# Ten of sixteen weight decodings of a second layer set beside the attention pairs, and a new room for four weights

## The chip, the cores and the metric

The kernel runs on one core of one Trainium2 chip. The metric is the device time of one execution in microseconds (us). Three executions of the kernel before took 651.32, 652.01 and 653.17 us; the median is 652.01 us. "A change of 0.3%" is about 2 us here.

## The reference

The program computes a causal attention with a compressive memory and then a two-layer network on its output.

```python
# q, k, v: (4, 8, 576, 64)   k is scaled by 8, z_prev by 8
scores = q @ k.T / 8, causal;  a = softmax(scores);  local = a @ v
q_p = elu(q) + 1
mem_out = (q_p @ M_prev) / (q_p . z_prev + 1e-6)
x = g * mem_out + (1 - g) * local          # g = sigmoid(beta), per head
x -> (2304 tokens, 512)
h = x @ w_in                               # (512, 2048)
out = (h * sigmoid(1.702 * h)) @ w_out     # (2048, 512)
```

Both weight matrices are 64-bit floats in memory. The kernel reads them as pairs of 32-bit words and decodes them to 32-bit floats on the chip.

## The kernel before, in words

**Stage one: pairs beside the first layer.** A pair is one batch index and two heads, so there are 16 pairs. `plan_prep` and `plan_attend` enter each step of a pair into a table of slots (`at(slot, priority, fn)`); `step()` runs one slot's entries and then issues matmuls of the first layer (`first_moe`) until the slot has its share of TensorE time (`PACE`). Pairs are 7 slots apart at first and 8 later: `K0` is 0, 7, 14, 21, 29, 37, ..., 61 for pair 8, ..., 117 for pair 15. The program text is then ordered again by a scheduler that simulates the engines' time and takes, per engine, what it believes is ready, by priority in order of text; an instruction can so stand earlier in its engine's queue than in the text. Each engine runs its queue in order.

The first layer runs over eight chunks of tokens (`chunks`: 256 and 320 columns for each batch index) and, in each chunk, over 16 blocks of 128 hidden units. A block is 12 matmuls (four of depth 128, each with a high and a low part of the weight and a low part of the activation). `gate` copies a finished block from PSUM into an SBUF tile `hk` (three buffers) and stores it into a scratch tensor `gd` in DRAM; the copies are ScalarE's in the late part, and alternate between VectorE and ScalarE before. Chunk 7's input tiles `xh`, `xl` lie in the pool `mop`.

**Decoding a weight block** of 128x512 numbers takes one load of 512 KB (`wraw`), one ScalarE scaling (`scale`), three VectorE bit operations (`bits`) and, later, a split in a high and a low part. First-layer weights are decoded by `conv_unit` (loads on SyncE's DMA queue), the second layer's by `conv_pair` (loads on GpSimd's DMA queue). A second-layer weight `wo` number kk (0 to 7) is made of two blocks, kk and kk+8; `sums` forms four sums and differences of their halves (tile `st`), `w_hi` copies raw halves and sums to the high part on ScalarE (three instructions), `w_lo` subtracts to get the low part on VectorE (three instructions). The seven products of a Strassen step use these parts. In the kernel before all sixteen blocks are decoded after the last pair, in the loop `while fill["gen"] is not None or conv_q or events`, beside the first layer's last chunks; weights 0 to 4 get their split in that loop, weights 5 to 7 after it.

**Stage two: the second layer.** `units` lists 84 units: three groups of 768 tokens, seven products, four parts p. Unit n needs weights 2p and 2p+1 and one tile `g` of activations: `load_g` loads 384 KB from `gd` on SyncE's queue, `gelu` applies the activation on ScalarE, `split` makes `oh` (ScalarE) and `ol` (VectorE) from it, `product` issues 12 matmuls. The first four units use tiles g[1,1] (p = 0 to 3), the next four g[0,0], then g[1,0], then g[0,1]. Two of the g[1,1] tiles have room of their own (`g11a`) and are loaded in the loop (k = 18 and 20).

**Room.** Pools stack up from two sides of SBUF in the order in which they are opened; a pool opened after another was closed takes its room, and a tile in it waits until the tiles that lay there are done. `left.close()` frees `mop` (23.75 KB in each partition), `cnv` (8 KB of raw words), and the first layer's 16 weights (4 KB each). On that room the second layer's pools are opened: in the kernel before g10 (12 KB), g01 (12), weights 5, 6, 7 (14 each), g11b (6), opb (6), g00 (12).

## Time and profile before

| | |
|---|---|
| profiled execution | 655.16 us, of which the span of its instructions is 653.1 us |
| median of three executions | 652.01 us |
| TensorE (PE) busy | 603.1 us, 92% of the span, 4000 matmuls |
| VectorE (DVE) busy | 417.1 us, 64% |
| ScalarE (ACT) busy | 355.2 us, 54% |
| GpSimd (POOL) busy | 164.0 us, 25% |
| mean granted TensorE clock | 0.98 |

The stages by the clock of the trace: first queries until about 45 us; pairs beside the first layer until 388 us; the first layer's rest until 450 us; the second layer to 648 us. Engines run their own queues in order, so an idle stretch of an engine is read by what ended it ("<-"). PEclk is the granted TensorE clock, 1.00 for 2.4 GHz and 0.50 for 1.2 GHz. Matmul ends are modelled, and neighbouring matmuls overlap in the rows; the start times are used for counting.

### The profile page before, as it was taken

What the parts mean: (1) busy time and instruction counts of PE and PEld (TensorE: products, weight loads), DVE (VectorE), ACT (ScalarE), POOL (GpSimd) and SP (SyncE); (2) the same over time, 40 slices, a digit from 0 to 9 for tenths busy, and PEclk for the clock granted to TensorE, in tenths of its full rate; (3) what the DMA queues carried; (4) which work ended last, traced back from release to release, by engine and by line L of the source; (5) the groups of instructions that cost most, each with busy time, mean ns of one, the idle gap of its engine ahead of it and who ended that gap; (6) DMA issues with size and microseconds to landing.
All of it is one profiled execution on the core that took longest, in us unless ns stands there. A gap on an engine that the chain in (4) does not pass through costs nothing.

```text
span 653.1 us, 11384 instructions
## 1 busy us (share of the span) xinstructions
PE 603.1 (92%) x4000; PEld 524.9 (80%) x4000; DVE 417.1 (64%) x1024; ACT 355.2 (54%) x817; POOL 164.0 (25%) x231
## 2 busy tenths in 40 slices
PE   3788998999999999999999989998299999999996
PEld 2547765688757888888888879998299999999996
DVE  4998766554667455446545434797696579449943
ACT  5765566544666445445544443557756764675451
POOL 3446644533455233333334200110000000000000
PEclk9989899999999999999999989998699999999999
DMA  8737552323323324224312144668605640671002
GB/s 249 251 118 264 169 164 93 126 65 115 118 88 120 101 77 136 84 93 135 109 68 75 46 151 139 215 239 249 225 0 170 176 140 19 202 206 58 24 2 73
DMA packets 54729, 84.11 MB, mean 129 GB/s; under 512 B 5392, under 2 KB 44816, under 8 KB 54672
## 3 DMA queue, kind: packets, MB, share of 16 engines
q1 hardware_dynamic: 52368, 75.00, 35.9%
q0 software_dynamic: 2304, 8.39, 4.0%
q8 instruction: 31, 0.51, 0.3%
q14 instruction: 26, 0.21, 0.1%
HBM read 59.77 MB, written 23.59 MB: 128 GB/s over the span
## 4 chain that ended last, share of the span: by engine, by line
PE 64%; DVE 11%; DMA 10%; ACT 9%; issue 4%; POOL 1%; SPq 1%; DVEq 0%; ACTq 0%; POOLq 0%
PE pm L124 26%; PE acc L875 14%; PE po L124 8%; PE ps L124 8%; PE pt L130 7%; DMA g<-gd 7%; DVE ol L143 3%; ACT oh L135 2%; ACT g L838 2%; DVE g L143 1%; DMA gd<-hk 1%; DVE ps L469 1%; ACT a L475 1%; ACT at L475 1%; DMA fq<-in_vq_dram 1%
## 5 line engine op out<-in xcount | busy, mean ns | idle before, releaser
L124 PE MATMUL pm<-xh,wi 128*128 128x320 f32 (+1 forms) x1024 | 216.9, 304 | 5.1 <-ACT hk L135 1.8
L875 PE MATMUL acc<-oh,wo 128*128 128x384 f32 x672 | 161.3, 342 | 15.3 <-ACT oh L135 12.3
L124 PEld LDWEIGHTS pm<-xh,wi 128*128 128x128 f32 x1024 | 165.8, 191 | 9.3 <-ACT hk L135 2.9
L124 PE MATMUL pm<-xl,wi 128*128 128x256 f32 (+1 forms) x512 | 153.2, 301 | 0.2 <-DVE xl L143 0.2
L875 PEld LDWEIGHTS acc<-oh,wo 128*128 128x128 f32 x672 | 122.0, 191 | 18.3 <-ACT oh L135 15.3
L143 DVE TENSOR_TENSOR ol<-g,oh 128x768 fp32r<-128x768 f32 x84 | 79.3, 954 | 52.7 <-ACT oh L135 50.0
L478 POOL TENSOR_SCALAR a<-a,sm,g 128x512 f32<-128x512 f32 (+3 forms) x112 | 70.2, 640 | 133.6 <-DVE sm L528 120.2
L469 DVE CUSTOM_DVE_ANT_0 ps<-ps,mask 128x256 f32<-128x256 f32 (+4 forms) x144 | 67.5, 507 | 52.5 <-PE ps L124 49.8
L875 PE MATMUL acc<-ol,wo 128*128 128x384 f32 x336 | 99.5, 340 | 0.4 <-DVE ol L143 0.3
L124 PEld LDWEIGHTS pm<-xl,wi 128*128 128x128 f32 x512 | 97.7, 191 | 1.6 <-DVE xl L143 1.3
L135 ACT ACTIVATE oh<-g 128x768 fp32r<-128x768 f32 x84 | 70.4, 841 | 48.6 <-PE acc L875 48.3
L475 ACT ACTIVATE a<-ps,nm 128x256 f32<-128x256 f32 (+2 forms) x112 | 59.9, 542 | 67.4 <-DVE nm L469 67.2
L124 PE MATMUL ps<-kqf 128*128 128x288 f32 (+4 forms) x288 | 67.7, 477 | 3.4 <-DVE xl L143 0.7
L875 PEld LDWEIGHTS acc<-ol,wo 128*128 128x128 f32 x336 | 62.5, 190 | 1.4 <-DVE ol L143 1.3
L135 ACT ACTIVATE hk<-pm 128x320 f32<-128x320 f32 (+1 forms) x82 | 32.8, 412 | 52.4 <-PE pm L124 31.4
L130 PE MATMUL pt<-ident,a 128*128 128x128 f32 x296 | 52.6, 273 | 0.0
L838 ACT ACTIVATE g<-g 128x768 f32<-128x768 f32 x48 | 39.9, 841 | 21.7 <-DMA g<-gd 20.3
L124 PEld LDWEIGHTS po<-e,vr 128*64 128x64 f32 x416 | 30.0, 137 | 20.0
L135 ACT ACTIVATE e<-pt 128x320 f32<-128x320 f32 (+2 forms) x76 | 32.9, 438 | 23.2 <-PE pt L130 19.9
L124 PE MATMUL po<-e,vr 128*64 128x320 f32 (+3 forms) x416 | 45.5, 359 | 0.0
L143 DVE TENSOR_TENSOR g<-g,g 128x768 f32<-128x768 f32 x48 | 44.3, 951 | 0.1
L124 PEld LDWEIGHTS ps<-kqf 64*128 64x128 f32 (+1 forms) x288 | 30.2, 188 | 17.0 <-issue 4.6
(120 smaller groups left out, 735.9 us busy)
## 6 DMA issues: line engine op xcount, KB each, us to landing
g<-gd SPq DMA_DIRECT2D x48, 384.0 KB, 3.9
gd<-hk SPq DMA_DIRECT2D x64, 160.0 KB, 1.9
wraw<-in_w_in_dram SPq DMA_DIRECT2D x16, 512.0 KB, 4.8
gd<-hk SPq DMA_DIRECT2D x64, 128.0 KB, 2.2
wraw<-in_w_out_dram POOLq DMA_DIRECT2D x16, 512.0 KB, 4.5
kqf<-in_kq_dram SPq DMA_DIRECT2D x12, 608.0 KB, 5.3
vr<-in_vq_dram SPq DMA_DIRECT2D x16, 320.0 KB, 4.4
qr<-in_vq_dram SPq DMA_DIRECT2D x12, 320.0 KB, 3.1
```

Source lines behind the costliest of these rows:

```text
L124: x = nc.tensor.matmul(out, l, r, start=start, stop=stop)
L130: nc.tensor.transpose(out, in_, idn)
L135: return nc.scalar.activation(out=dst, in_=src, func=AF.Copy, **kw)
L143: return (nc.vector if eng == "V" else nc.gpsimd).tensor_tensor(out=dst, in0=a, in1=b, op=op)
L469: nc.vector.tensor_tensor_reduce(out=ps, in0=ps, in1=mk, op0=ALU.add, op1=ALU.min, scale=-0.125, scalar=1e38 if j == 0 else nm[:, j - 1:j] ...
L475: return nc.scalar.activation(out=a, in_=ps, func=AF.Exp, scale=-1.0, bias=nm, accum_out=sm)
L478: (nc.vector if eng == "V" else nc.gpsimd).tensor_scalar(out=a, in0=a, scalar1=r, scalar2=gcol, op0=ALU.mult, op1=ALU.mult)
L838: nc.scalar.activation(out=t, in_=t, func=AF.Gelu_apprx_sigmoid)
L875: nc.tensor.matmul(acc[b, j][:, :QN], W[2 * p + kk][:, WPART[i], sp, 128 * j:128 * j + 128], mv[:, kk], start=first and p + kk == 0 and sp ...
```

## The change

Ten of the sixteen second-layer blocks (weights 2, 3, 5, 6, 7, list `HERE`) are decoded by a new function `decode` at slots 60, 64, ..., 96, beside pairs 8 to 12: the load is issued from SyncE's queue and waits for the last softmax exponential issued so far, the scaling and the bit operations come four slots later and now write to SBUF, into tiles `r`. The room for them: two tiles that held raw words of first-layer weights (`ear[0]`), and three tiles that later hold sums of the second layer (`ear[1]`, which replaces `snp`). `fq` and `fv` of the first queries move into the input tiles' pool `mox`. The loop after the pairs decodes the other three weights (order 0, 4, 1, 2, 3; one weight every third step); weights 0 to 3 get sums and split in it, weights 4 to 7 after it. First-layer weights 14 and 15 move next to `mop`, and after `left.close()` the order is g10, g01, g00, g11b, opb and then weights 4 to 7. The largest of the three subtractions of `w_lo` goes to GpSimd for weights 0 to 3. In the late part every third block's `hk` copy goes to VectorE. Each `gelu` now waits for the last `hk` copy issued before it; those of g[1,1] with p = 2, 3 wait for the seventh from the last only. The first two are issued at k = 9 and 11.

```diff
     cst = pool(ctx, "cst", side="left")
     mop = pool(left, "mop", 2, side="left")
+    w1 = {k: pool(left, f"w1_{k}", side="left") for k in (NB - 1, NB - 2)}
     cnv = pool(left, "cnv", side="left")
-    w1 = [pool(left, f"w1_{k}", side="left") for k in range(W0)]
+    w1.update({k: pool(left, f"w1_{k}", side="left") for k in range(W0)})
+    ear = [pool(left, "ear", 2, side="left")]
+    ear.append(pool(ctx, "rl", 3, side="right"))
...
-        xq[n] = [p.tile([128, NK, XW], F32R, name=x) for x in ("xh", "xl")]
+        xq[n] = [p.tile([128, NK, XW], F32R, name=x, tag=x) for x in ("xh", "xl")]
...
-        q = fst.tile([128, NP, 2, 128], F32, name="fq")
+        q = mox.tile([128, NP, 2, 128], F32, name="fq", tag="xh")
-        v = fst.tile([128, NP, 2, 128], F32, name="fv")
+        v = mox.tile([128, NP, 2, 128], F32, name="fv", tag="xl")
...
+            state["exp"] = x.ins.name
...
+    late_hk = []
             h = mop.tile([128, XW], F32, name="hk", bufs=3)
-            copy("AV"[blk % 2 == 0 and len(moe_ps) == 1], h[:, :w], ps[:, :w])
+            x = copy("AV"[blk % (2 if len(moe_ps) == 1 else 3) == 0], h[:, :w], ps[:, :w])
+            state["hk"] = x.ins.name
+            late_hk.append(state["hk"])
             nc.sync.dma_start(gd[blk // 2][blk % 2, :, t0:t0 + w], h[:, :w])
...
-        raw = (att, {"tag": "W1", "bufs": 2}) if other else (cnv, {"bufs": 2})
+        raw = (ear[0], {"tag": "r"}) if other else (cnv, {"bufs": 2})
...
-    w1 += [pool(left, f"w1_{k}", side="left", reuse_waits="tile") for k in range(W0, NB)]
+    w1.update({k: pool(left, f"w1_{k}", side="left", reuse_waits="tile") for k in range(W0, NB - 2)})
...
+    KK = NB // 2
+    EARLY = 4
+    HERE = (2, 3, 5, 6, 7)
+    raw2 = {}
+
+    def bit_ops(raw, si, r):
+        nc.vector.tensor_scalar(out=si, in0=si, scalar1=3, scalar2=None, op0=ALU.logical_shift_left)
+        nc.vector.scalar_tensor_tensor(
+            out=si, in0=raw[:, :, 1], scalar=-2 ** 31, in1=si, op0=ALU.bitwise_and, op1=ALU.bitwise_or)
+        nc.vector.scalar_tensor_tensor(
+            out=r, in0=raw[:, :, 0], scalar=29, in1=si, op0=ALU.logical_shift_right, op1=ALU.bitwise_or)
+
+    def decode(i):
+        kk, h = HERE[i // 2], i % 2
+        if h == 0:
+            raw2[kk] = ear[kk > EARLY].tile([128, 2, DM], F32, name="r", tag="r")
+        raw = cnv.tile([128, DM, 2], I32, name="wraw", bufs=2)
+        r = raw2[kk][:, h]
+        x = nc.sync.dma_start(raw.rearrange("p f w -> p (f w)"), w_out[kk + KK * h].bitcast(I32))
+        tc.add_manual_dep(x.ins, state["exp"], SYNC, reason="not yet")
+
+        def scale():
+            x = nc.scalar.activation(out=r, in_=raw[:, :, 1].bitcast(F32), func=AF.Copy, scale=2.0 ** -112)
+            tc.add_manual_dep(x.ins, state["exp"], NOSYNC, reason="not yet")
+
+        at(state["slot"] + 4, 56, scale)
+        at(state["slot"] + 4, 57, lambda: bit_ops(raw, r.bitcast(I32), r.bitcast(I32)))
+
+    for i in range(2 * len(HERE)):
+        at(60 + 4 * i, 58, lambda i=i: decode(i))
...
-    EARLY = 5
     g11a = pool(ctx, "g11a", 2, side="right", reuse_waits="tile")
+    u2s = pool(ctx, "u2s", side="right", reuse_waits="tile")
     stage = ExitStack()
     stg = pool(stage, "stg", 2, side="right", reuse_waits="tile")
...
     def w_lo(kk):
         for w, src in wparts(kk):
             hi, lo = (w[:, 0], w[:, 1]) if len(w.shape) == 3 else (w[:, :, 0], w[:, :, 1])
-            sub("V", lo, src, hi)
+            sub("P" if kk < EARLY and len(w.shape) == 4 and w.shape[1] == 4 else "V", lo, src, hi)
+
+    def sums(kk):
+        st = st2[kk] = stg.tile([128, 4, DH], F32, name="st")
+        ra, rb = raw2[kk][:, 0], raw2[kk][:, 1]
+        tt("V", st[:, 0], ra[:, DH:], rb[:, DH:], ALU.add)
+        tt("V", st[:, 1], st[:, 0], ra[:, :DH], ALU.subtract)
+        tt("V", st[:, 2], ra[:, :DH], ra[:, DH:], ALU.subtract)
+        tt("V", st[:, 3], rb[:, :DH], st[:, 1], ALU.subtract)
     def conv_pair(kk):
...
-        at(s0 + 3, 60, sums)
+            raw = cnv.tile([128, DM, 2], I32, name="wraw", bufs=2)
+            nc.gpsimd.dma_start(raw.rearrange("p f w -> p (f w)"), w_out[kk + KK * h].bitcast(I32))
+            if h == 0:
+                raw2[kk] = stg.tile([128, 2, DM], F32, name="r")
+
+            def words():
+                s = ps_w.tile([128, DM], F32, name="ws", tag="pm2")
+                nc.scalar.activation(out=s, in_=raw[:, :, 1].bitcast(F32), func=AF.Copy, scale=2.0 ** -112)
+                bit_ops(raw, s.bitcast(I32), raw2[kk][:, h].bitcast(I32))
+
+            at(s0 + 2, 60, words)
+
+        if kk not in HERE:
+            for h in range(2):
+                at(s0, 5, lambda h=h: load(h))
         if kk < EARLY:
+            at(s0 + 3, 60, lambda: sums(kk))
             at(s0 + 4, 40, lambda: new_w(w2a, kk))
             at(s0 + 4, 41, lambda: w_hi(kk))
             at(s0 + 4, 42, lambda: w_lo(kk))
...
     def gelu(kh, th, p):
         t = G[kh, th, p]
-        nc.scalar.activation(out=t, in_=t, func=AF.Gelu_apprx_sigmoid)
+        x = nc.scalar.activation(out=t, in_=t, func=AF.Gelu_apprx_sigmoid)
+        if "hk" in state:
+            tc.add_manual_dep(x.ins, state["hk"], SYNC, reason="not yet")
...
     def save(name, b, j):
-        t = snap[name, j] = pools["snp"].tile([128, QN], F32, name=f"{name}{j}")
-        copy("A", t, acc[b, j][:, :QN])
+        if j == 0:
+            kw = {"tag": "u"} if name == "u2" else {"tag": "r"}
+            snap[name] = (u2s if name == "u2" else ear[1]).tile([128, 2, QN], F32, name=name, **kw)
+        copy("A", snap[name][:, j], acc[b, j][:, :QN])
...
-    conv_q = list(range(KK))
+    conv_q = [0, 4, 1, 2, 3]
     k = 0
     while fill["gen"] is not None or conv_q or events:
         k += 1
-        if (k % 5 in (2, 4) or fill["gen"] is None) and conv_q:
+        if (k % 3 == 1 or fill["gen"] is None) and conv_q:
             conv_pair(conv_q.pop(0))
-        if k in (18, 20):
-            at(state["slot"] + 1, 5, lambda p=(k - 18) // 2: load_g(0, 1, 1, p))
-            at(state["slot"] + 4, 50, lambda p=(k - 18) // 2: gelu(1, 1, p))
+        if k in (9, 11):
+            at(state["slot"] + 1, 5, lambda p=(k - 9) // 2: load_g(0, 1, 1, p))
+            at(state["slot"] + 4, 50, lambda p=(k - 9) // 2: gelu(1, 1, p))
         step()
     left.close()
     pools[1, 0] = pool(ctx, "g10", 4, side="left", reuse_waits="tile")
     pools[0, 1] = pool(ctx, "g01", 4, side="left", reuse_waits="tile")
-    w2b = [pool(ctx, f"w2_{kk}", side="left", reuse_waits="tile") for kk in range(EARLY, KK)]
+    pools[0, 0] = pool(ctx, "g00", 4, side="left", reuse_waits="tile")
     pools[1, 1] = pool(ctx, "g11b", 2, side="left", reuse_waits="tile")
     pools["op", 1] = pool(ctx, "opb", side="left", reuse_waits="tile")
-    pools[0, 0] = pool(ctx, "g00", 4, side="left", reuse_waits="tile")
+    w2b = [pool(ctx, f"w2_{kk}", side="left", reuse_waits="tile") for kk in range(EARLY, KK)]
     for kk in range(EARLY, KK):
+        sums(kk)
         new_w(w2b[kk - EARLY], kk)
         w_hi(kk)
         w_lo(kk)
...
+    last, state["hk"] = state["hk"], late_hk[-7]
     gelu(1, 1, 2)
     gelu(1, 1, 3)
+    state["hk"] = last
```

## Rows read from the trace of the kernel before

**Rows 1.** Waits of PE after 440 us: us in total, times, longest.
```profile
PE acc L875 <- ACT oh L135: 12.3, 2, 11.7
PE acc L875 <- ACT hk L135: 2.6, 1, 2.6
```

**Rows 2.** Stretches; columns: us, busy of PE, PEld, DVE, ACT, POOL, PEclk, DMA share, GB/s.
```profile
449.90:458.60 8.70, 6.08 (x25) 5.44 (x23) 8.09 (x15) 6.88 (x13) 0.00 (x0) 0.80 0.85 261
458.60:470.30 11.70, 0.00 (x1) 0.00 (x1) 6.34 (x12) 11.16 (x16) 0.00 (x0) 0.71 0.75 267
470.30:474.00 3.70, 3.70 (x12) 3.70 (x13) 3.63 (x4) 1.41 (x2) 0.00 (x0) 0.53 0.00 0
```

**Rows 3.** The chain that ended last, after 619 us: start, us, what.
```profile
619.09 28.17 PE acc L875 x160
```

**Rows 4.** The same chain, 441 to 467 us.
```profile
441.06 7.52 DMA g<-gd
...
459.10 6.22 DMA g<-gd
...
465.54 1.04 ACT wo L135
466.58 0.73 ACT oh L135
```

**Rows 5.** Timeline of ScalarE, 382 to 386 us.
```profile
382.13 1.28 ACT L838 ACT_TABLE_LOAD   x1 [2.06 <-DMA g<-gd]
383.43 0.85 ACT L838 ACTIVATE g<-g 128x768 f32<-128x768 f32 x1
...
385.85 0.42 ACT L135 ACTIVATE xh<-po 128x320 fp32r<-128x320 f32 x1
```

**Rows 6.** Timeline of PE at the same place.
```profile
386.93 0.65 PE L124 MATMUL po<-qpt,ms 128*64 128x256 f32 x4 [2.06 <-DVE xl L143]
388.17 0.71 PE L124 MATMUL pm<-xh,wi 128*128 128x320 f32 x2
...
392.01 0.45 PE L124 MATMUL pm<-xh,wi 128*128 128x320 f32 x2
...
392.44 0.45 PE L124 MATMUL pm<-xh,wi 128*128 128x320 f32 x2
```

**Rows 7.** Groups by line, 376 to 471 us: busy us, mean ns, idle before.
```profile
L135 ACT ACTIVATE hk<-pm 128x320 f32<-128x320 f32 (+1 forms) x39 | 15.1, 412 | 24.3 <-PE pm L124 13.2 <-DMA gd<-hk 9.5 <-issue 1.3
L791 ACT ACTIVATE ws<-wraw 128x512 f32<-128x512 f32 x16 | 9.8, 631 | 0.1
L797 DVE SCALAR_TENSOR_TENSOR ws<-wraw,ws 128x512 int32<-128x512 int32 x16 | 10.7, 688 | 0.0
```

**Rows 8.** DMA issues of the page: count, KB each, us to landing.
```profile
g<-gd SPq DMA_DIRECT2D x48, 384.0 KB, 3.9
```

**Rows 9.** Stretches of the pairs (columns as in rows 2).
```profile
60.00:100.00 40.00, 37.77 (x253) 28.68 (x251) 28.59 (x81) 24.12 (x63) 21.85 (x25) 0.96 0.55 167
...
185.00:200.00 15.00, 13.77 (x99) 9.10 (x101) 10.97 (x42) 9.99 (x32) 8.39 (x11) 1.00 0.28 96
200.00:296.00 96.00, 95.66 (x720) 79.94 (x720) 50.57 (x181) 46.64 (x139) 34.62 (x45) 1.00 0.33 106
```

**Rows 10.** Groups by line of VectorE, 60 to 100 us (columns as in rows 7).
```profile
L215 DVE SCALAR_TENSOR_TENSOR wr<-wraw,ws 128x512 int32<-128x512 int32 x6 | 4.1, 681 | 0.1
```

**Rows 11.** Waits of PE, 60 to 100 us (columns as in rows 1).
```profile
PE pm L124 <- ACT wi L135: 1.1, 1, 1.1
```

**Rows 12.** Waits of SyncE's DMA queue, 185 to 296 us (columns as in rows 1).
```profile
SPq L667 <- ACT hk L135: 27.2, 13, 5.7
```

**Rows 13.** Timeline of VectorE, one operation twice: start, us, what.
```profile
23.13 1.64 DVE L424 SCALAR_TENSOR_TENSOR qp<-qr,qmt 128x384 f32<-128x384 f32 x1
...
45.56 0.55 DVE L424 SCALAR_TENSOR_TENSOR qp<-qr,qmt 128x384 f32<-128x384 f32 x1
```

**Rows 14.** Timeline of GpSimd at the first of the two.
```profile
22.95 1.41 POOL L143 TENSOR_TENSOR wi<-wr,wi 128x512 fp32r<-128x512 f32 x1 [0.48 <-ACT wi L135]
```

More of the change, by code (lines that the diff above doesn't have):

```diff
@@ L744, in tile_attention_memory_moe @@
     moe_ps.append((ps_w, "pm2"))
-    KK = NB // 2
-    EARLY = 5
     QN = 384
@@ L752, in tile_attention_memory_moe @@
     g11a = pool(ctx, "g11a", 2, side="right", reuse_waits="tile")
+    u2s = pool(ctx, "u2s", side="right", reuse_waits="tile")
     stage = ExitStack()
     stg = pool(stage, "stg", 2, side="right", reuse_waits="tile")
-    W, raw2 = {}, {}
+    W, st2 = {}, {}
     def wparts(kk):
-        ra, rb, st = raw2[kk]
+        ra, rb = raw2[kk][:, 0], raw2[kk][:, 1]
         w = W[kk]
-        return ((w[:, 0], ra[:, :DH]), (w[:, 1:3], rb.rearrange("p (c f) -> p c f", c=2)), (w[:, 3:7], st))
+        return ((w[:, 0], ra[:, :DH]), (w[:, 1:3], rb.rearrange("p (c f) -> p c f", c=2)), (w[:, 3:7], st2[kk]))
     def new_w(p, kk):
@@ L773, in w_lo @@
             hi, lo = (w[:, 0], w[:, 1]) if len(w.shape) == 3 else (w[:, :, 0], w[:, :, 1])
-            sub("V", lo, src, hi)
+            sub("P" if kk < EARLY and len(w.shape) == 4 and w.shape[1] == 4 else "V", lo, src, hi)
+    def sums(kk):
+        st = st2[kk] = stg.tile([128, 4, DH], F32, name="st")
+        ra, rb = raw2[kk][:, 0], raw2[kk][:, 1]
+        tt("V", st[:, 0], ra[:, DH:], rb[:, DH:], ALU.add)
+        tt("V", st[:, 1], st[:, 0], ra[:, :DH], ALU.subtract)
+        tt("V", st[:, 2], ra[:, :DH], ra[:, DH:], ALU.subtract)
+        tt("V", st[:, 3], rb[:, :DH], st[:, 1], ALU.subtract)
@@ L776, in conv_pair @@
     def conv_pair(kk):
-        box = {}
         s0 = state["slot"] + 1
-        def room():
-            raw2[kk] = [stg.tile([128, DM], F32, name=f"r{h}") for h in range(2)]
-            raw2[kk].append(stg.tile([128, 4, DH], F32, name="st"))
-        at(s0 + 2, 59, room)
         def load(h):
-            box["raw", h] = (cnv, stg)[kk % 2].tile([128, DM, 2], I32, name="wraw", bufs=2)
-            nc.gpsimd.dma_start(box["raw", h].rearrange("p f w -> p (f w)"), w_out[kk + KK * h].bitcast(I32))
@@ L789, in scale @@
-        def scale(h):
-            box["s", h] = ps_w.tile([128, DM], F32, name="ws", tag="pm2")
-            nc.scalar.activation(
-                out=box["s", h], in_=box["raw", h][:, :, 1].bitcast(F32), func=AF.Copy, scale=2.0 ** -112)
-        def bits(h):
-            raw, si, r = box["raw", h], box["s", h].bitcast(I32), raw2[kk][h]
-            nc.vector.tensor_scalar(out=si, in0=si, scalar1=3, scalar2=None, op0=ALU.logical_shift_left)
-            nc.vector.scalar_tensor_tensor(
-                out=si, in0=raw[:, :, 1], scalar=-2 ** 31, in1=si, op0=ALU.bitwise_and, op1=ALU.bitwise_or)
-            nc.vector.scalar_tensor_tensor(
-                out=r.bitcast(I32), in0=raw[:, :, 0], scalar=29, in1=si,
-                op0=ALU.logical_shift_right, op1=ALU.bitwise_or)
@@ L803, in sums @@
-        def sums():
-            ra, rb, st = raw2[kk]
-            tt("V", st[:, 0], ra[:, DH:], rb[:, DH:], ALU.add)
-            tt("V", st[:, 1], st[:, 0], ra[:, :DH], ALU.subtract)
-            tt("V", st[:, 2], ra[:, :DH], ra[:, DH:], ALU.subtract)
-            tt("V", st[:, 3], rb[:, :DH], st[:, 1], ALU.subtract)
-        for h in range(2):
-            at(s0, 5, lambda h=h: load(h))
-            at(s0 + 2, 60, lambda h=h: scale(h))
-            at(s0 + 2, 61, lambda h=h: bits(h))
-        at(s0 + 3, 60, sums)
+            raw = cnv.tile([128, DM, 2], I32, name="wraw", bufs=2)
@@ L853, in save @@
     def save(name, b, j):
-        t = snap[name, j] = pools["snp"].tile([128, QN], F32, name=f"{name}{j}")
-        copy("A", t, acc[b, j][:, :QN])
+        if j == 0:
+            kw = {"tag": "u"} if name == "u2" else {"tag": "r"}
+            snap[name] = (u2s if name == "u2" else ear[1]).tile([128, 2, QN], F32, name=name, **kw)
+        copy("A", snap[name][:, j], acc[b, j][:, :QN])
     def join(gr, name, b, j, mh, th):
-        t = snap[name, j]
+        t = snap[name][:, j]
         tt("V", t, acc[b, j][:, :QN], t, ALU.add)
@@ L917, in tile_attention_memory_moe @@
     pools["op", 2] = pool(ctx, "opc", side="right", reuse_waits="tile")
-    pools["snp"] = pool(ctx, "snp", side="right", reuse_waits="tile")
     pools["ps"] = pool(ctx, "ps_a", 8, space=PSUM, side="left", reuse_waits="tile")
```

## The prediction

> **What bounds the kernel now.** I read the page's slices first, then the waits of PE, then busy time by stretch, then the chain that ended last. PE is busy nearly throughout; it stands in the first 45 us (the first queries, which the change leaves alone), for a moment near 385 us, and where the first layer ends and the second begins.
>
> That last place is the large one. After 440 us PE waits 12.3 us for `oh` and 2.6 us for an `hk` copy, the longest waits being 11.7 and 2.6 us [rows 1]. From 449.9 to 474.0 us, 24.1 us, PE does three units (25 and 12 matmul records, of 36 that three units hold) [rows 2]; at the pace of the run's end, 160 matmuls in 28.17 us [rows 3], a unit of 12 takes 2.11 us and three take 6.3. So 17.8 us go here: 14.3 standing, the rest at a low clock. The granted clock is 0.71 in the stretch in which PE stood and 0.53, that is the 1.2 GHz level, in the 3.7 us after it [rows 2].
>
> The chain says why PE stood. ScalarE's queue holds a `gelu` whose tile is still being loaded (441.06 us, 7.52 us); `hk` copies and further weight work stand behind it. Then come a load of 6.22 us from 459.10, weight splits and gelus, and only at 466.58 the `oh` of the third unit [rows 4]. In these 11.7 us ScalarE is busy for 11.16 [rows 2]: it is the engine that sets the start of the second layer, with the weights' splits, the gelus and `oh` in one queue. DMA moves 267 GB/s meanwhile at a busy share of 0.75 [rows 2].
>
> The small place has the same form: at 382 us ScalarE, which waited 2.06 us for a `g` tile, loads the table for gelu (1.28 us) and runs a gelu; `xh` follows only at 385.85 [rows 5]. PE stands 2.06 us for what depends on it, and its next matmuls run slowly: five triples from 388.17 to 392.01 us take 3.84 us where a later one takes 0.43 (392.01 to 392.44), so 2.15: 1.7 us [rows 6].
>
> **The change part by part**, against the profiled execution (655.16 us: 653.1 of span and 2.1 around it; it is 3.15 above the median of 652.01).
>
> *Gelus held back until an `hk` copy.* The first two can no longer stand before the last pair's `xh`. The stall near 385 us goes: 2.06 + 1.7 = 3.8 us. What is late next: the table load and two gelus (1.28 + 2 x 0.85 = 3.0 us) now fall between `hk` copies of the later chunks. A block is 12 matmuls, four triples of 0.43 us or 1.7 us, and there are eight PSUM banks for blocks and words, so two banks more cover the 3.0 us. Without that cover it would cost up to 3.0 - 1.7 = 1.3. I take -3.7 us, bounds -3.8 and -2.5. What is queued behind the waiting gelu on ScalarE are `hk` copies and splits of weights; they wait for the same `hk` copy's matmuls anyway.
>
> *The ten decodings that leave the end.* Each block is one ScalarE instruction of 0.63 us and three on VectorE of 0.68 to 0.69 [rows 7]: 6.3 and 20.7 us less between 376 and 471 us. Of PE's time this is worth nothing while PE is full (until 450 us), and everything in the 17.8 us after it. A third of 39 `hk` copies also leaves ScalarE: 13 x 0.41 = 5.3 us [rows 7].
>
> *Four weights with room of their own.* From the tile sizes, the new order on the left side (counted from the start of `mop`) is g10 0 to 12 KB, g01 to 24, g00 to 36, g11b to 42, opb to 48, weights 4 to 7 to 62, 76, 90 and 104. Below them lay `mop` to 23.75 KB, first-layer weights 15 and 14 to 31.75, `cnv` to 39.75, weights 0 to 5 to 63.75, `ear[0]` to 71.75, weights 6 to 13 to 103.75. So g11b and opb are free once `cnv` and weights 0 and 1 are, far ahead; weight 4 after the last chunk's block 5, weight 5 after block 7, weight 6 after block 10, weight 7 after block 13, two blocks (3.5 us) before the first layer's end. Its split, three ScalarE instructions of at most 1.04 us [rows 4] and three on VectorE, ends near that end and is needed three units later. So the third and fourth units should find their weights and their `oh`.
>
> What then remains at the border: the last `hk` copy (0.41 [rows 7], 0.6 with its hand-over), after which the PSUM banks and all other gelus are free; and the loads. g10 and g01 lie where chunk 7's inputs were, g00 partly where weights 14 and 15 were, so these twelve loads of 384 KB start only at the border. At the 267 GB/s of [rows 2] one is 1.47 us, and landing takes 3.9 [rows 8], so load n is there about 1.47 n + 2.4 us after the border. The fifth unit starts 0.6 + 4 x 2.11 = 9.0 us after it, and gelu and `oh` (0.85 for the gelu [rows 5], about the same for `oh`) need 1.7 us before. In the order of the text the first g00 is load 1 (3.9 us, needed at 7.3), the fourth is load 7 (12.7, needed at 13.6): in time. The first g10 is load 9: 15.6 us, needed at 9.0 + 8.4 - 1.7 = 15.7: just. I add 1.2 us for jitter of these loads and one gelu of 0.8 that stands ahead of a needed `oh`: 2.6 us remain. Lower bound 0.6; upper, if the units can't go on before all twelve are in: 12 x 1.47 + 3.9 - 8.4 = 13.1. I take 2.6, since the loads fit by the nearest rows. Gain: 17.8 - 2.6 = 15.2 us (bounds 17.2 and 4.7).
>
> *The ten decodings beside pairs 8 to 12* (slots 60 to 100; by the repeating pattern of the pairs about 187 to 296 us). VectorE gets 20.7 us on 61.5, ScalarE 6.3 on 56.6, of 111 us [rows 9], so both have room. Where PE has first-layer work (200 to 296 us, 95.66 of 96 busy) it is covered by that. Where it has little (185 to 200 us, 13.77 of 15 busy, VectorE 10.97), two decodings meet a bare chain of score, maximum, exponential. The nearest case is 60 to 100 us, where the last decoding step stands six times beside pairs [rows 10]: PE is idle 2.23 us in all [rows 9], 0.37 for each, or 0.19 without the 1.1 us in which it waits for a first-layer weight itself [rows 11]. I take 10 x 0.28 = +2.8 us, between the two. Bounds: -1.6 (all the idle time of 185 to 296 us gone through another order), and 10 x (0.63 + 3 x 0.69) = +27 if each stands in the chain with its full length.
>
> The load of a decoding waits for an exponential on SyncE's queue. Behind it stand `hk` stores and the next pair's loads. Stores there wait 27.2 us in 13 times for ScalarE's `hk` copies already, up to 5.7 us [rows 12], without PE noticing; `hk` has three buffers. So nothing for this, within the bounds above.
>
> A rule that speaks against the change: a VectorE instruction with two SBUF inputs can be held up by GpSimd. The row: `qp<-qr,qmt` over 384 columns takes 0.55 us at 45.56 us and 1.64 at 23.13, where a GpSimd subtraction of 1.41 us had begun 0.18 us before [rows 13, 14]. The Trainium skill, "SBUF — State Buffer", section "Who interferes with whom", says that such an instruction takes the read port which GpSimd uses, and that the loser waits for the winner's whole instruction. The trace agrees, with 1.1 us. In the old form the two combining operations read one input from PSUM; now they read both from SBUF, and GpSimd is busy 43.0 of these 111 us [rows 9]. By that rule it is the rival below.
>
> *Moves of `fq`, `fv`, the joined `snp` tiles, sums after the loop, the subtraction on GpSimd:* nothing. The first two are read before chunk 1 writes their buffer; sums and splits of weights 4 to 7 run while PE works off the last chunk, and GpSimd is idle after 376 us. If that cover failed, it is the third rival.
>
> *Sum:* -3.7 - 15.2 + 2.8 = -16.1 us. Own time 655.2 - 16.1 = 639.1; against the median 652.0 - 16.1 = 635.9, so **636 us**.
>
> **The rivals.**
> 1. *The border stays bound by loads and gelus.* Twelve gelus (10.2 us) and thirteen `oh` (11 us), with six saves, fill ScalarE's queue over 25 us, and it already waits for `g` loads today (the 7.52 us of [rows 4] begin so). For: the loads fit by only 0.1 us at the first g10. Against: the order of units gives 8.4 us before the first load counts. PE would stand some 8 us more and fall to the low clock once (1.7): 636 + 9.7, **646 us**.
> 2. *GpSimd and VectorE hold each other up in the pairs.* Thirty new instructions with SBUF operands, 39% of them meeting GpSimd, 1.1 us each: 12.9 us, half of it landing on PE: **642 us**.
> 3. *The border is not freed, so the change does not do what it says*: the scheduler puts the four weights' sums and splits late, and the third unit waits as before. Only the small stall goes: 652 - 3.7 + 2.8, **651 us**. For: four weights' sums and splits now stand behind the loop, three splits before. Against: their rooms are free 3.5 to 17 us ahead of the border.
> 4. *Slower than before:* the decodings stand in the chain of the pairs. VectorE's queue is strictly in order; 2.1 us in front of a maximum (or an exponential behind a scaling) delay a pair's scores. With the full 27 us it is 652 - 18.9 + 27 = **660 us**. It decides from 18.9 / 10 = 1.9 us per decoding on PE. Against: 0.19 to 0.37 in the nearest case.
>
> **How the numbers follow.** Forecast 0.58, rival 1 0.20, rival 2 0.08, rival 3 0.06, rival 4 0.08. About 2 us (0.3%) is what a measurement can tell from no change. Faster: 0.58 + 0.20 + 0.08 and a part of rival 3, 0.02: 0.88; the same 0.04; slower 0.08. The range takes in the forecast with its bounds (629 with border and pairs near their good ends) and rivals 1 and 2, and ends at 648 us; rivals 3 and 4 lie beyond it.
>
> **What would show it.** Right: PE's wait for `oh` at the border under 3 us and the clock there at 1.00; no gelu on ScalarE before the last `xh`, and no idle time of PE near 385 us; PE full from 200 to 296 us, with at most 3 us more until pair 12. Wrong: long waits of PE for `oh` 9 to 25 us into the second layer with ScalarE waiting for `g` loads (rival 1); bit operations of more than 0.8 us beside GpSimd work (rival 2); the wait at the border for `wo` (rival 3); first-layer end later than before by over 5 us (rival 4).

## The result and the profile after

The changed kernel takes 641.0 us (median of 4 executions, 639.33 to 642.24) against 651.66 us (650.97 to 653.17): a ratio of 0.9832, 95% interval 0.9802 to 0.9861, so 9 to 13 us less. The forecast was 636 us, with a range of 629 to 648. The profiled execution of the changed kernel took 640.63 us (span 638.9), like its median; that of the kernel before, 655.16 us, was 3.5 us above the 651.66 us here, so the two spans differ by more (14.2 us) than the medians (10.7 us).

First the border between the layers in the changed kernel: waits of PE from 430 to 480 us (us in total, times, longest), then the stretches that answer to [rows 2] (columns as there).

```profile
PE acc L907 <- ACT oh L138: 3.0, 2, 1.8
PE acc L907 <- DVE ol L146: 1.2, 2, 1.0
```

```profile
446.98:458.60 11.62, 9.77 (x55) 9.14 (x54) 5.64 (x8) 7.14 (x11) 0.00 (x0) 1.00 0.89 291
458.60:470.30 11.70, 9.31 (x50) 8.20 (x49) 10.94 (x13) 11.51 (x17) 0.00 (x0) 1.00 0.51 181
470.30:474.00 3.70, 3.70 (x23) 3.70 (x23) 3.70 (x5) 1.68 (x4) 0.00 (x0) 1.00 0.00 0
```

The one wait of 11.7 us of [rows 1] is gone, and in this profile the low clock with it: it is 1.00 in all three stretches, where [rows 2] has 0.80, 0.71 and 0.53. A second profile of the changed kernel (e0_changed_again below) has waits for `oh` of 4.0 us in sum, and for two microseconds behind them the clock is at the 1.2 GHz level:

```profile
460.30:462.30 2.00, 2.00 (x8) 2.00 (x7) 0.82 (x1) 1.92 (x3) 0.00 (x0) 0.50 1.06 391
```

So of the signs that the forecast gave for being right, a wait under 3 us and a clock of 1.00, the first was missed in both profiles (3.0 and 4.0) and the second in one. From the first matmul of the second layer to the end of the span it is 191.9 us (446.98 to 638.9) against 203.3 before (449.8 to 653.1), 11.4 us less; the forecast had 15.2. The rest of the difference of the spans, 2.8 us, lies ahead of the border.

The chain of the changed kernel at the border (start, us, what) shows what is late now, and two timelines show why: SyncE's queue and ScalarE.

```profile
447.14 2.12 PE acc L907 x12
449.27 0.31 SPq L862
...
450.69 0.42 SPq L862
...
451.16 6.54 DMA g<-gd
...
458.48 0.84 ACT oh L138
...
461.24 0.82 issue
462.06 0.95 DVE g L146
463.01 0.87 DVE ol L146
```

```profile
449.20 0.93 SPq L862 DMA_DIRECT2D g<-gd  x2
450.22 0.42 SPq L675 DMA_DIRECT2D gd<-hk  x1
450.69 7.40 SPq L862 DMA_DIRECT2D g<-gd  x10
```

```profile
449.44 0.85 ACT L138 ACTIVATE oh<-g 128x768 fp32r<-128x768 f32 x1 [0.68 <-DVE wo L146]
453.61 0.84 ACT L866 ACTIVATE g<-g 128x768 f32<-128x768 f32 x1 [3.32 <-DMA g<-gd]
454.35 0.83 ACT L138 ACTIVATE oh<-g 128x768 fp32r<-128x768 f32 x1
```

The first matmul of the second layer runs at 446.98, but the loads of the next `g` tiles begin only at 449.20, and ten of the twelve stand behind the store of the last `hk`, which leaves at 450.22. So the first gelu on such a tile starts at 453.61, after a wait of 3.32 us, and a copy to `oh` whose own tile had been ready since 443.5 stands behind it: this is PE's 1.8 us. Behind it the chain goes through a load of 6.5 us, then a gelu and its `oh`, and then VectorE's subtractions of gelus that stand in front of an `ol`.

The pairs, 185 to 296 us, in the stretches of [rows 9], and the decodings' three operations there (groups by line, 185 to 330 us: busy us, mean ns, idle before):

```profile
185.00:200.00 15.00, 12.84 (x91) 8.41 (x89) 12.05 (x44) 10.49 (x32) 8.56 (x11) 1.00 0.49 166
200.00:296.00 96.00, 95.08 (x714) 79.34 (x711) 66.69 (x204) 49.99 (x147) 41.80 (x47) 1.00 0.48 153
```

```profile
L755 DVE SCALAR_TENSOR_TENSOR r<-wraw,r 128x512 int32<-128x512 int32 x10 | 9.4, 938 | 0.2
L757 DVE SCALAR_TENSOR_TENSOR r<-wraw,r 128x512 int32<-128x512 int32 x10 | 8.7, 872 | 0.1
L754 DVE TENSOR_SCALAR r<-r 128x512 int32<-128x512 int32 x10 | 4.8, 481 | 1.1 <-ACT r L770 1.1
```

PE is idle 2.16 + 0.92 = 3.1 us there, 1.6 before [rows 9]: the ten decodings cost some 1.5 us. (It is 3.0 to 3.8 us in the other seven profiles with the ten decodings there once, and 1.6 to 2.0 in the four without them.) The combining operations take 938 and 872 ns, where six of the same form, reading from PSUM late in the same kernel, take 686 and 679.

### The profile page after: what moved, and what is told of

Same layout as the page of the kernel before. It is cut to its first block, busy times and chain, and to the rows that moved or that the text cites. A ratio compares the mean times of both kernels' runs of the same rounds, so it can differ in the third digit from the quotient of the medians.

```text
span 638.9 us, 11382 instructions
## 1 busy us (share of the span) xinstructions
PE 599.4 (94%) x4000; PEld 518.7 (81%) x4000; DVE 425.6 (67%) x1034; ACT 348.0 (54%) x803; POOL 176.6 (28%) x225
## 4 chain that ended last, share of the span: by engine, by line
PE 64%; DVE 13%; DMA 8%; ACT 7%; issue 5%; POOL 2%; SPq 1%; DVEq 0%; ACTq 0%; POOLq 0%
PE pm L127 29%; PE acc L907 12%; PE po L127 8%; PE ps L127 7%; PE pt L133 7%; DMA g<-gd 6%; DVE ol L146 3%; DVE g L146 2%; ACT oh L138 2%; DVE ps L472 1%; ACT a L478 1%; ACT g L866 1%; POOL qmt L146 1%; DMA kqf<-in_kq_dram 1%; DMA fq<-in_vq_dram 1%
## 5 line engine op out<-in xcount | busy, mean ns | idle before, releaser
L127 PE MATMUL pm<-xh,wi 128*128 128x320 f32 (+1 forms) x1024 | 214.3, 302 | 4.9 <-DVE hk L141 1.7
L127 PEld LDWEIGHTS pm<-xh,wi 128*128 128x128 f32 x1024 | 163.5, 189 | 8.8 <-DVE hk L141 2.3
L907 PE MATMUL acc<-oh,wo 128*128 128x384 f32 x672 | 159.0, 338 | 4.9 <-ACT oh L138 4.6
L907 PEld LDWEIGHTS acc<-oh,wo 128*128 128x128 f32 x672 | 119.7, 188 | 7.9 <-ACT oh L138 7.9
L146 DVE TENSOR_TENSOR ol<-g,oh 128x768 fp32r<-128x768 f32 x84 | 80.8, 971 | 54.8 <-ACT oh L138 54.7
L481 POOL TENSOR_SCALAR a<-a,sm,g 128x512 f32<-128x512 f32 (+3 forms) x112 | 78.6, 712 | 121.9 <-DVE sm L532 92.9
L127 PEld LDWEIGHTS pm<-xl,wi 128*128 128x128 f32 x512 | 96.1, 188 | 1.8 <-DVE xl L146 1.6
L138 ACT ACTIVATE hk<-pm 128x256 f32<-128x256 f32 (+1 forms) x68 | 27.8, 412 | 44.4 <-PE pm L127 31.3
L141 DVE COPY hk<-pm 128x256 f32<-128x256 f32 (+1 forms) x60 | 27.1, 451 | 27.8 <-PE pm L127 22.3
```

What stands on the lines that cost most here:

```text
L127: x = nc.tensor.matmul(out, l, r, start=start, stop=stop)
L138: return nc.scalar.activation(out=dst, in_=src, func=AF.Copy, **kw)
L141: return nc.vector.tensor_copy(dst, src)
L146: return (nc.vector if eng == "V" else nc.gpsimd).tensor_tensor(out=dst, in0=a, in1=b, op=op)
L481: (nc.vector if eng == "V" else nc.gpsimd).tensor_scalar(out=a, in0=a, scalar1=r, scalar2=gcol, op0=ALU.mult, op1=ALU.mult)
L907: nc.tensor.matmul(acc[b, j][:, :QN], W[2 * p + kk][:, WPART[i], sp, 128 * j:128 * j + 128], mv[:, kk], start=first and p + kk == 0 and sp ...
```

## The experiments

**Theory** after these profiles: the gain is the hold-back of the gelus (the stall near 385 us) and the border, freed by moving the ten decodings; what is missing of the forecast lies in the order on ScalarE at the border. **Rivals**: the rooms or the hold-back free the border, wherever the decodings stand; the loads of `g` bound the border whatever the order; GpSimd's subtractions cost something. Ratios are to the kernel before, executed beside each set. A difference between ratios of 0.003 is 2 us, about what can be told.

**e3_hold_only**: the kernel before, with the hold-back alone (the lines that note the `hk` copies are left out here).

```diff
...
+        if "hk" in state:
+            tc.add_manual_dep(x.ins, state["hk"], SYNC, reason="not yet")
```

> The kernel before with the hold-back of the gelus alone. Theory: the stall near 385 us goes, -3.8 us, and the border stays as it was (17.8 us lost, PE waits of 10 to 12 us in one piece for oh), so about 648 us (0.994 to 0.995 of the kernel before). Rival A: the held gelus come later to a border that is already behind, and give the 3.8 us back: 651 to 653 us, border loss 20 us or more. Rival B: the hold-back is what frees the border: 641 us or less.

Measured 647.4 us, 0.9934 (0.9912 to 0.9957): 4.3 us less, by the theory. PE is busy 12.0 of 12 us from 376 to 388 us (9.94 in the kernel before), and still waits 13.1 us for `oh` at the border. The hold-back alone does not free it.

```profile
376.00:388.00 12.00, 12.00 (x91) 10.24 (x91) 5.52 (x11) 3.63 (x8) 0.00 (x0) 1.00 0.38 135
```

```profile
PE acc L881 <- ACT oh L135: 13.1, 2, 9.8
```

**e2_no_hold**: the changed kernel without those two lines.

> The changed kernel without the dependency that makes the gelus wait for a stored hk; all else as changed. Theory (the hold-back is worth the stall near 385 us and no more): the early gelus stand again before xh on ScalarE, PE idles about 2 us there and runs about 1.7 us longer at the lower clock, so 641.0 + 3.8 = about 645 us (0.989 of the kernel before); the border after the first layer stays as in the changed kernel (waits of PE for oh below 5 us in sum). Rival A (the hold-back also frees the border, since gelus that wait for nothing would stand between the conversions of weights): 650 us, and PE waits over 8 us for oh behind the first layer's end. Rival B (the stall had another cause, the moved decodings or the second room): 641 us, PE busy 12.0 of 12 us from 376 to 388 us.

Measured 639.35 us, 0.9822 (0.9798 to 0.9846): nothing was lost, and the theory's 645 us is wrong. ScalarE's timeline of this kernel says why; compare [rows 5].

```profile
378.60 1.28 ACT L866 ACT_TABLE_LOAD   x1 [2.31 <-DMA g<-gd]
379.89 1.58 ACT L866 ACTIVATE g<-g 128x768 f32<-128x768 f32 x2
...
381.75 0.43 ACT L138 ACTIVATE xh<-po 128x320 fp32r<-128x320 f32 x1
```

The change also asks for the first two `g` tiles at steps 9 and 11 of the loop, not 18 and 20. So the table load and both gelus are over by 381.47, `xh` follows at 381.75 where [rows 5] has it at 385.85, and PE stands 0.49 us instead of 2.06. In e8_no_hold_order, which has the same early loads and no hold-back either, the tile came later and PE stood 1.57 us, so the early loads do not always prevent the stall. By the times, the edit is worth 4.3 us in the old order and nothing that can be told from noise in the new one.

**e4_late_words**: the changed kernel, the ten decodings put back beside the late loop.

```diff
-    for i in range(2 * len(HERE)):
-        at(60 + 4 * i, 58, lambda i=i: decode(i))
...
-        if kk not in HERE:
-            for h in range(2):
-                at(s0, 5, lambda h=h: load(h))
+        for h in range(2):
+            at(s0, 5, lambda h=h: load(h))
...
-    conv_q = [0, 4, 1, 2, 3]
+    conv_q = list(range(KK))
...
-        if (k % 3 == 1 or fill["gen"] is None) and conv_q:
+        if (k % 5 in (2, 4) or fill["gen"] is None) and conv_q:
```

> The changed kernel with all ten decodings taken out of the pairs and put back beside the late loop, their loads and words as for the other weights, with rooms, hold-back and GpSimd's subtractions as changed. Theory (moving the ten decodings frees the border): the border's loss comes back almost whole, 11.6 us, less the 0.8 us that the decodings cost in the pairs: about 652 us (1.000 of the kernel before), PE's waits for oh or wo behind 447 us over 10 us. Rival A (rooms of their own and held gelus free the border, wherever the decoding stands): 640 to 642 us, and 185:200 and 200:296 back at 13.8 and 95.7 us busy. Rival B (the decodings in the pairs cost more than the stretches show): 637 us.

Measured 656.1 us, 1.0082 (1.0057 to 1.0107): rival A falls, and the loss is larger than the theory's 652 us. PE waits 7.4 us for an `hk` copy on VectorE and 8.9 us for `oh`. But this kernel has two rooms for raw words, where the kernel before has four, and its loads stand on GpSimd's queue behind the subtractions. So it was taken apart further, in two steps.

**e10_late_words_rooms**: as e4_late_words, with more rooms for raw words and all subtractions of weights on VectorE. By the code the rooms are two and three, not the four of the expectation; the kernel before has two and two.

```diff
...
-            raw = cnv.tile([128, DM, 2], I32, name="wraw", bufs=2)
+            raw = (ear[1].tile([128, DM, 2], I32, name="wraw", tag="r") if kk % 2 else
+                   cnv.tile([128, DM, 2], I32, name="wraw", bufs=2))
```

> The ten decodings beside the late loop again, as in e4_late_words, and now with four rooms for raw words, as the kernel before has them, and with all lower halves of the second layer's weights on VectorE; the hold-back and the four weights' own rooms stay as changed. Theory (moving the decodings frees the border, and e4_late_words was slower than the kernel before by what it took away besides: two of four rooms for raw words, and loads queued on GpSimd behind its subtractions): the hold-back's 3.7 us and nothing else, about 647 us (0.994 of the kernel before), PE's waits of 2.6 to 12 us behind the first layer's end as before. Rival A (the rooms of their own for four weights carry a part of the gain): 642 to 645 us. Rival B (raw words' rooms and GpSimd's queue had no part in e4_late_words' loss): 654 to 657 us.

Measured 654.0 us, 1.0037 (1.0014 to 1.0061): at the near end of rival B's range, and far from the theory's 647. By the ratios it is 2.9 us below e4_late_words, so the rooms and GpSimd's queue had a part in that loss, but a small one. On VectorE work follows work nearly without a gap from 415 to 461 us, a third of the late `hk` copies stand in that queue, and the loads of `g` start at 455.12, 5.2 us after the border.

**e13_late_words_hk_act**: e10_late_words_rooms with those copies on ScalarE, as before the change.

```diff
...
-            x = copy("AV"[blk % (2 if len(moe_ps) == 1 else 3) == 0], h[:, :w], ps[:, :w])
+            x = copy("AV"[blk % 2 == 0 and len(moe_ps) == 1], h[:, :w], ps[:, :w])
```

> As e10_late_words_rooms (the ten decodings beside the late loop, four rooms for raw words, lower halves on VectorE), and all late hk copies on ScalarE, as the kernel before has them. Theory (in e10_late_words_rooms VectorE was busy without a gap from 418 to 461 us, and the last hk copy stood in its queue, so that the stores and the loads of g came late; that ate the hold-back's gain): 647 to 649 us (0.994 of the kernel before), the last hk stored before 452 us. Rival A (VectorE's own work on the weights ends last, wherever hk is copied): 652 to 655 us, PE waits 10 us or more for oh. Rival B (four weights' own rooms carry a gain of their own once hk is out of the way): 643 to 645 us.

Measured 649.3 us, 0.9959 (0.9936 to 0.9982): within 0.4 us of the theory. The loads start at 449.30, and PE still waits 11.6 us for `oh`:

```profile
PE acc L905 <- ACT oh L138: 11.6, 1, 11.6
PE acc L905 <- DVE r L757: 1.7, 1, 1.7
```

So with rooms, hold-back and early loads, and the decodings late, the border is as it was: the rooms alone give nothing. A third of the `hk` copies on VectorE costs 5 us (e10 against e13) while VectorE still has the decodings; what those copies give or cost in the changed kernel no run shows.

**e0_changed_again** and **e5_sub_on_dve**: the changed kernel once more, and with this edit:

```diff
-            sub("P" if kk < EARLY and len(w.shape) == 4 and w.shape[1] == 4 else "V", lo, src, hi)
+            sub("V", lo, src, hi)
```

> The changed kernel itself, beside the other three of this set, as the measure for them and for e5_sub_on_dve. Theory (its 641.0 us is its time): 640 to 642 us (0.983 of the kernel before), so that e5_sub_on_dve (0.977) is about 4 us faster. Rival (641.0 was a high draw of four executions): 637 to 639 us, and the subtractions on VectorE gain nothing.

> The changed kernel with the four big subtractions of the weights' lower halves on VectorE instead of GpSimd (four of 2.5 us there, about 1.2 us each on VectorE). Theory (they cost and give nothing, as the forecast had it): 641 us (0.983 of the kernel before), PE's waits at the border within 1 us of the changed kernel's. Rival A (VectorE's 4.9 us more delay the last hk and ol copies at the border): 643 to 645 us. Rival B (beside GpSimd's subtraction VectorE's and ScalarE's work on the same weights stretches and waits, one took 2.89 us): 638 to 640 us.

Measured: the changed kernel 639.9 us, 0.9826 (0.979 to 0.9861); with all subtractions on VectorE 636.5 us, 0.9773 (0.9742 to 0.9804). The first took what its theory said; the second went the way of rival B, and further than the 638 to 640 us given there. The two intervals overlap by 0.0014. But five of the six executions of e5_sub_on_dve lie below all nine of the changed kernel (lowest 639.33 us), and e14_dve_order below, also with these subtractions on VectorE, takes 636.6 us. Both traces of the changed kernel show the same cause. VectorE and then GpSimd in the changed kernel:

```profile
399.34 3.56 DVE L146 TENSOR_TENSOR wo<-r,wo 128x256 fp32r<-128x256 f32 x3
...
425.54 2.96 DVE L146 TENSOR_TENSOR st<-r 128x256 f32<-128x256 f32 x2 [2.88 <-POOL wo L146]
...
433.02 2.54 DVE L146 TENSOR_TENSOR ol<-g,oh 128x768 fp32r<-128x768 f32 x1 [1.12 <-ACT oh L138]
```

```profile
399.51 2.50 POOL L146 TENSOR_TENSOR wo<-st,wo 128x1024 fp32r<-128x1024 f32 x1 [7.99 <-ACT wo L138]
...
423.11 4.78 POOL L146 TENSOR_TENSOR wo<-st,wo 128x1024 fp32r<-128x1024 f32 x2 [13.01 <-ACT wo L138]
432.33 2.41 POOL L146 TENSOR_TENSOR wo<-st,wo 128x1024 fp32r<-128x1024 f32 x1 [4.45 <-ACT wo L138]
```

And VectorE in e5_sub_on_dve, the same operations:

```profile
427.49 0.76 DVE L146 TENSOR_TENSOR st<-r 128x256 f32<-128x256 f32 x2
...
429.65 1.23 DVE L146 TENSOR_TENSOR wo<-st,wo 128x1024 fp32r<-128x1024 f32 x1 [1.07 <-ACT wo L138]
...
436.89 0.95 DVE L146 TENSOR_TENSOR ol<-g,oh 128x768 fp32r<-128x768 f32 x1
...
449.76 0.48 DVE L141 COPY hk<-pm 128x320 f32<-128x320 f32 x1
```

An `ol` of 0.95 us takes 2.54 and two `st` of 0.76 take 2.96 while GpSimd subtracts, and `ol` ends at 435.56, 0.8 us after GpSimd's instruction did (432.33 + 2.41). The sums by form on VectorE, 388 to 453.7 us (busy us, mean ns, idle before), the changed kernel first and e5_sub_on_dve behind it:

```profile
L146 DVE TENSOR_TENSOR st<-r 128x256 f32<-128x256 f32 x16 | 8.2, 554 | 3.0 <-POOL wo L146 2.9
L146 DVE TENSOR_TENSOR wo<-r,wo 128x512 fp32r<-128x512 f32 x8 | 7.7, 957 | 0.0
L146 DVE TENSOR_TENSOR ol<-g,oh 128x768 fp32r<-128x768 f32 x3 | 4.4, 1482 | 1.7 <-ACT oh L138 1.7
```

```profile
L146 DVE TENSOR_TENSOR st<-r 128x256 f32<-128x256 f32 x16 | 6.0, 420 | 0.1
L146 DVE TENSOR_TENSOR wo<-r,wo 128x512 fp32r<-128x512 f32 x8 | 5.5, 687 | 0.0
L146 DVE TENSOR_TENSOR ol<-g,oh 128x768 fp32r<-128x768 f32 x3 | 2.9, 952 | 0.5 <-ACT oh L138 0.5
```

In the changed kernel the same three groups take 5.9 us more, and VectorE waits another 2.9 us until a subtraction of GpSimd is done; the four subtractions that it is spared are 4.9 us. The stretch 388 to 447 us (columns as in [rows 2]) shows the same, the changed kernel first:

```profile
388.00:447.00 59.00, 58.85 (x437) 58.65 (x436) 44.04 (x81) 29.63 (x56) 11.91 (x8) 1.00 0.40 134
```

```profile
388.00:447.00 59.00, 59.00 (x440) 59.00 (x439) 43.99 (x88) 30.62 (x57) 2.18 (x4) 1.00 0.40 136
```

VectorE is busy as long with the four subtractions (43.99 us) as without them (44.04). In the changed kernel it starts to copy the last `hk` at 449.27, 2.3 us after PE's first second-layer matmul (4.8 us in e0_changed_again: 453.13 against 448.3); in e5_sub_on_dve at 449.76, 0.6 us after it (449.15). Its store and ten loads of `g` follow that copy. In e5_sub_on_dve PE's waits for `oh` at the border are gone, and 2.7 us for `ol` remain:

```profile
PE acc L907 <- DVE ol L146: 2.7, 3, 1.1
```

From the first second-layer matmul to the end it is 186.9 us, against 191.9 in both profiles of the changed kernel. This difference is a weak measure, since single executions scatter as much: in the first of the two profiles 1.6 us of it is a wait of PE at 574 us, far behind the border; e2_no_hold, with the subtractions on GpSimd, has 187.2 in an execution 3.6 us below its own median; and e14_dve_order has 189.5. The size of the effect is taken from the executions, some 3.6 us.

**e7_oh_first**: gelus of the first `g00` tiles one unit later on ScalarE, behind the latest `oh` copy.

```diff
-        if s == 0:
+        if gr == 0:
+            if 1 <= n <= 4:
+                gelu(0, 0, n - 1, state["oh"])
+        elif s == 0:
             gelu(0, 0, p)
...
```

> The changed kernel with the gelus of the first g00 tiles standing one unit later on ScalarE, behind the oh copy of the unit before: oh of unit 3, ready to go, no longer stands behind a gelu that waits 3.3 us for its load. Theory (the shortfall of the forecast at the border is ScalarE's order): PE's wait of 1.8 us at 455 us goes or falls below 0.5, the first s join comes 1 to 2 us earlier, 639 to 640 us (0.981 of the kernel before). Rival A (the load of g00 is what ends last: the unit after waits in its place): 641 us, the wait of 1.5 to 2.5 us moves from unit 3 to unit 4. Rival B (the later gelus push oh at 464 to 467 us back): 642 to 644 us.

Measured 640.65 us, 0.9835 (0.9813 to 0.9856). The 1.8 us at 455 us went, and waits of 0.98, 0.92 and 0.44 us came from 461 us on. The time is rival A's, though the waits are smaller and later than it said. This order is not what the forecast lacked.

**e8_no_hold_order** and **e14_dve_order**: e7_oh_first, with gelus of `g01` and `g10` behind the `oh`, and subtractions of gelus behind the `ol`, of the unit after; the first without the hold-back, the second with it and with all weight subtractions on VectorE.

```diff
+            b = state["ohs"][n + 1] if gr == 0 else None
...
-            gelu(1, 0, p)
-            diff((0, 1), (0, 0), (0, 0), p)
+            gelu(1, 0, p, b)
+            diff((0, 1), (0, 0), (0, 0), p, state["ols"][n + 1] if gr == 0 else None)
```

> The changed kernel without the hold-back of the gelus, with the order of e7_oh_first, and in the first group the gelus of g01 and g10 behind the oh copy of the unit after, and the subtractions of the gelus behind that unit's ol. Theory (what is left at the border is the order on ScalarE and VectorE: ready oh and ol copies stand behind gelus and subtractions that nobody needs yet): PE's waits from 447 to 475 us below 2 us in sum, against 4.2 us in the changed kernel, 637 to 638.5 us (0.979 of the kernel before). Rival A (both engines are full there, and what is put off is late next): the waits move on to 475 to 490 us, 640 to 642 us. Rival B (without the hold-back the table load and the early gelus cost PE their stall again): PE below 10.5 of 12 us busy from 376 to 388, 643 us or more.

> The changed kernel with the weights' big subtractions on VectorE (e5_sub_on_dve) and the order of e8_no_hold_order at the border, the hold-back kept. Theory (the two gains are of different waits and add: GpSimd's hold on VectorE, and gelus and subtractions of gelus ahead of oh and ol): 634 to 636 us (0.974 of the kernel before), PE's waits for ol behind 450 us below 1.5 us against 2.7 in e5_sub_on_dve. Rival A (with GpSimd out, VectorE and ScalarE are full at the border and the order has nothing left to give): 636 to 637.5 us. Rival B (the order puts off gelus that are late next): 638 us or more.

Measured 638.8 us, 0.981 (0.9783 to 0.9836), and 636.6 us, 0.9763 (0.9723 to 0.9803). The first is not told apart from the changed kernel, the second not from e5_sub_on_dve (its rival A): the order gives nothing that can be told here.

**e9_old_order**: the late weights' rooms ahead of those for `g11b`, operands and `g00`.

> The changed kernel with the rooms behind the loop in the old order: the four late weights' rooms ahead of those of g11b, the operands and g00, and g00's last. Theory (which room an early load waits for decides when g00 lands: the weights take the space that comes free first and g00 waits for more of the loop's rooms): the load of g00 lands later than 453.6 us, PE waits longer than 1.8 us for oh there, 642 to 646 us. Rival A (all of these rooms come free together at the loop's end, the order is of no weight): 641 us, waits within 0.5 us of the changed kernel's. Rival B (the weights' rooms come earlier and the border gains): 638 to 640 us.

Measured 642.65 us, 0.9857 (0.9831 to 0.9884), 1.6 to 2 us slower by the ratios, the least that can be told here. The time is the theory's, but the way is not: the `g00` loads leave from 447.49 on, earlier than in the changed kernel (449.20). The two of `g11b` leave at 439.77 instead of 422.11; weight conversions and four gelus then stand ahead of the next `oh`, and PE waits once, 7.4 us.

**e15_decode_twice**: each of the ten decodings' scaling and bit operations done twice beside the pairs.

```diff
+        at(state["slot"] + 4, 58, scale)
+        at(state["slot"] + 4, 59, lambda: bit_ops(raw, r.bitcast(I32), r.bitcast(I32)))
```

> The changed kernel with the scaling and the three bit operations of each of the ten moved decodings done twice, the second time over the first: 30 more operations on VectorE and 10 more on ScalarE beside pairs 8 to 12, no more loads. Theory (VectorE and ScalarE have room there, and what GpSimd and VectorE hold each other up hardly lands on PE: the first ten cost 0.8 us by PE's busy time from 185 to 296 us): 1 to 3 us more than the changed kernel, 642 to 644 us. Rival A (the decodings stand in the chain of the pairs, 1.9 us each): 655 us or more. Rival B (as the forecast priced them, 0.28 us each): 643.5 to 645 us. Rival C (they cost nothing, the 0.8 us is scatter): 641 us.

Measured 640.95 us, 0.9845 (0.9811 to 0.988), 1 us above the changed kernel of its set. PE is idle 4.8 us from 185 to 296 us, 1.7 more than in the changed kernel: a second ten cost what the first did (1.5 by the stretches above; the expectations' 0.8 is too low). Rival A falls; time alone can't part theory and rival C.

## Why the prediction was right, and where it was not

The measured 641 us lies half way between the forecast's 636 and rival 1's 646, so the time alone does not say whose mechanism it was. Put in order, the runs make a ladder in the forecast's own steps (us: difference of ratios by 651):

| step | forecast | measured | from |
|---|---|---|---|
| gelus held back | -3.7 | -4.3 | before, e3_hold_only (1, 0.9934) |
| rooms, early loads, decodings still late | 0 | +1.6, within measurement | e13_late_words_hk_act (0.9959) |
| ten decodings beside the pairs, a third of `hk` on VectorE (one step, not parted) | -15.2 + 2.8 = -12.4 | -12.1 | e5_sub_on_dve (0.9773) |
| big subtractions on GpSimd | 0 | +3.6 | changed kernel (0.9832 and 0.9826, mean 0.9829) |
| sum | -16.1 | -11.1 | |

*Border:* right in place and, without GpSimd's subtractions, in size; the cause was half named. Taking the decodings out frees it, and no other part does so by itself (e3, e13). The forecast called ScalarE the engine that sets the start of the second layer; the runs show VectorE's queue as much: with the decodings late, the `hk` copies in it cost 5 us (e10 against e13), and in the changed kernel the last `hk` copy, behind which the loads stand, comes late through it. Of the 17.8 us lost there, the forecast left 2.6; by the time from the first second-layer matmul to the end, e5_sub_on_dve leaves 1.4 and the changed kernel 6.4, each by single profiles.

*The step that failed* is the term that put "the subtraction on GpSimd" at nothing, with "GpSimd is idle after 376 us" as its cover; it measured +3.6 us. That cover was there; who pays is VectorE. The forecast had the mechanism in hand, with [rows 13, 14], but applied it to the pairs alone. By the Trainium skill, "SBUF — State Buffer", section "Who interferes with whom", a VectorE instruction with two SBUF inputs and a GpSimd instruction that reads SBUF contend for a port pair that one of them holds as an exclusive lock; the trace agrees, with 2.54 us for 0.95.

*Pairs:* +2.8 us was forecast; PE is idle 1.5 us more, and 1.7 us more again with ten more decodings (e15). Rival 2's own sign is there, bit operations of 938 ns beside GpSimd and GpSimd's 128x512 scalings of 1082 ns (773 before), but VectorE has room in the pairs and PE hardly sees it: its 12.9 us were far too many. Rival 4 falls with e15, rival 3 with PE's 1.8 us as its longest wait at the border.

*Rival 1* came true in part: the loads of `g` are on the chain, 6.5 us long under twelve at once where [rows 8] had 3.9. Ten of the twelve stand behind the store of the last `hk`, whose copy the forecast had done 0.6 us behind the border; in the changed kernel it is done 2.8 us behind it (449.27 + 0.48 against 446.98).

*Hold-back:* right as an edit of the kernel before. In the changed kernel it is worth nothing that the times show, and in the profile of e2_no_hold the earlier loads have done most of its work (0.49 us of PE's 2.06 left); so its term and the others do not simply add.

Open: why the profiled execution of the kernel before was some 3 us above its median. In the profiles of all these kernels the first layer ends between 444.0 and 451.8 us, and in the two of the changed kernel at 447.0 and 448.3, so some microseconds of the first 450 differ from execution to execution. The granted clock of the first 60 us differs too, from 0.74 (e15, whose first layer ends last) to 1.00 (e13), but does not put the others in order.

## What to carry to other kernels

Work given to an idle engine is free only if it takes nothing from its neighbour: look at what VectorE does while GpSimd would run, and if those instructions read two tensors from SBUF, count GpSimd's duration against VectorE. Find the stretch in which the queue that sets the next stage is full, and move out of it whatever can be done where its engines have room; here ten decodings cost 1.5 us in the pairs, and the step as a whole gave 12. The fastest versions run, e5_sub_on_dve (636.5 us) and e14_dve_order (636.6), are the change without its subtractions on GpSimd.

## What the runs showed of the hardware

A 128x1024 subtraction takes 1.22 us on VectorE and 2.4 to 2.5 us on GpSimd, and two VectorE subtractions of 128x256 that take 0.76 us without it took 2.96 beside it and ended 0.6 us after it. In the pairs both sides take longer: VectorE's combining operations 938 and 872 ns for 686 and 679 (those read one input from PSUM), and GpSimd's 128x512 scaling 1082 for 773. The shift of 128x512 int32 with one tensor input goes the other way: 694 ns (six, on PSUM) and 481 (ten, on SBUF, beside GpSimd's work).
